# Down products of a routed expert layer with w2 held in TensorE and the activations streamed, results turned by VectorE and put back into rows through DRAM

## Chip, cores and metric

One NeuronCore of a Trainium2 chip runs the whole program. The metric is device microseconds (us) from start to end of one execution; lower is better. An execution's own time is a little longer than the span that the profile covers, which goes from the first to the last instruction of the program.

## What is computed

A recurrence per head gives rows `x` (3072 tokens of 384 numbers), and an expert layer with one expert per token follows. Only the second part is touched:

```python
logits = x @ w_gate + modality_bias[modality_id]
e_idx = argmax(logits, axis=1)
...
for e in range(8):
    mask = e_idx == e
    h = maximum(x[mask] @ w1[e], 0)               # 384 -> 1024
    out[mask] = gate_w[mask, None] * (h @ w2[e])  # 1024 -> 384
```

With the inputs used, 2663 tokens go to one expert, 409 to another, and none to the other six.

## The kernel before, in words

Until about 122 us the recurrence runs in 24 steps. Its rows are scattered by expert to a DRAM buffer `xs` (GpSimd, L635), and a table in SBUF (`table`, L512) says for each block of rows which expert it has, where it starts, and whether its expert differs from that of the block before (`tab[:, 2]`). The expert layer then runs over `seq` (L892): blocks 0 to 4 of 512 rows, block 5 of 416 rows (the narrow block, `BQ`), and half a block (`HO`, 128 rows). With these inputs blocks 0 to 4 and the half block have the large expert, and block 5 the small one.

Each block has an up stage (`blk_up`, L699) and a down stage (`blk_down`, L720), both in eight steps f of 128 hidden columns. Each fp32 product is made of three fp32r products: a rounded part and a rest of either operand (`wh`, `wl` of the weights; `xh`, `xo` and `hh`, `hl` of the activations). The **up** stage holds a 128x128 piece of w1 in TensorE and streams the block's 512 (or 416) columns: 9 matmuls a step. Its result goes to one of three PSUM banks in turn (`UPB`, L697), so step f reuses the bank of step f-3. ScalarE makes `hh` from it (L714) and VectorE `hl` (L716). The **down** stage holds 128 columns of `hh` or `hl` in TensorE and streams 384 columns of w2: 3 matmuls for each of 4 groups of 128 rows, 12 a step, into the banks pY, pX, pK and pU. The narrow block has three such groups and 32 rows left, for which two matmuls with 64 and 32 held columns do (L732, L733); `blk_sum` adds their two halves. Right after the down stage `blk_out` (L743) scales each group on ScalarE straight from PSUM into `ot` (L756), and GpSimd scatters `ot` to the rows of the output (L747).

The schedule is written by hand: every engine runs its instructions in the order in which the program issues them. What stands around the blocks:

- `w_split` (L223): ScalarE rounds two steps' worth of the next block's weights into `wh` (L225), then VectorE (w1) or GpSimd (w2; VectorE in block 0 and the last) makes `wl` (L226). For w1 it stands behind steps f = 1, 3, 5, 7 of the up stage, in block 1 behind f = 0, 2, 4, 6 of its down stage; for w2 behind f = 1, 3, 5, 7 of the down stage.
- `blk_raw` (L644): SyncE (SP) loads the weights of a block ahead into `raw[0]` (w1) and `raw[1]` (w2), each in two halves, if the expert differs; if not, the load is issued with a false condition. For k = 0 SP first reads two values of `tab` (L646, L647). Block 3's `raw[0]` is issued after the down stage of block 1 (L964); those of later blocks stand ahead of a down stage (L942).
- `rows_load` (L652): SP loads a block's rows into `xl` with four DMAs of 192 KB in pieces of 384 bytes. `blk_t` (L671), issued at f = 0 of the block before's down stage, turns them with three VectorE transposes (L666) and makes `xh` and `xo`.
- `guard` (L400): eight checks of the decay inputs on ScalarE, two passes each (L403, L404), spread over blocks 2 to 5 by a step count `s` (`tend`, L882).

Of the kernel before, what the change touches and what calls it, by code (L numbers as in the profile page):

```python
# [9 lines left out]
F32 = mybir.dt.float32  # L10
# [24 lines left out]
NA = 2  # L35
NB = 4
NQ = NA + NB
NBX = 8
NH = 1
NHX = E * (JT - 1)  # L40
# [18 lines left out]
def kernel(ctx: ExitStack, tc: tile.TileContext, rkw, vt, wf, cst, mid, wg, bias, w1, w2, out):  # L59
# [3 lines left out]
    dp = ctx.enter_context(tc.tile_pool(name="dp", bufs=1, space=bass.MemoryType.DRAM))  # L63
    ps = ctx.enter_context(tc.tile_pool(name="ps", bufs=1, space=bass.MemoryType.PSUM))
    xs = dp.tile([XROWS, XW], F32, name="xs")


    cp.tile([P, 32], F32, name="pad0")
# [443 lines left out]
    def table(ph):  # L512
# [12 lines left out]
        def rows(o, nb, cu, f, base, unit=BT):  # L525

            sh = [P, nb, E]
            bc = lambda v: v[:, None, :].to_broadcast(sh)
            ib = ibk[:, 0:nb]
            at = C_EQ if ph == 0 else 0  # L530
            cm, c2 = rcol(at, nb, E), rcol(at + nb * E, nb, E)
            ct = C_TAB if ph == 0 else 2 * nb * E
            te, tr = rcol(ct, nb), rcol(ct + nb, nb)
            t2 = wt((ph, o), "t2", [P, NHX], 1)[:, 0:nb]
            tt(out=cm, in0=bc(cu[:, 1:E + 1]), in1=ib[:, :, None].to_broadcast(sh), op=ALU.is_le)
            vec.tensor_reduce(out=te, in_=cm, axis=AX.X, op=ALU.add)
            if f is not None:
                tt(out=c2, in0=cm, in1=bc(f), op=ALU.mult)
                vec.tensor_reduce(out=tr, in_=c2, axis=AX.X, op=ALU.add)
                tt(out=t2 if base is None else tr, in0=ib, in1=tr, op=ALU.subtract)  # L540
            if base is not None:
                t = rcol(ct + 2 * nb, nb)
                ts(out=t, in0=te, scalar1=-float(E), scalar2=None, op0=ALU.add)
                tt(out=cm, in0=bc(i8), in1=t[:, :, None].to_broadcast(sh), op=ALU.is_equal)
                tt(out=c2, in0=cm, in1=bc(base), op=ALU.mult)
                vec.tensor_reduce(out=t2, in_=c2, axis=AX.X, op=ALU.add)
                if f is not None:
                    tt(out=t2, in0=tr, in1=t2, op=ALU.add)
            yield

            vec.scalar_tensor_tensor(out=tr, in0=te, scalar=float(RS // unit), in1=t2, op0=ALU.mult, op1=ALU.add)
            ts(out=tab[:, 1, o:o + nb], in0=tr, scalar1=float(unit), scalar2=float(DUMMY), op0=ALU.mult, op1=ALU.min)
            es = tabe[:, o:o + nb]
            ts(out=es, in0=te, scalar1=float(E - 1), scalar2=None, op0=ALU.min)
            ts(out=tab[:, 0, o:o + nb], in0=te, scalar1=float(E - 1), scalar2=None, op0=ALU.min)
            prev = e0f if o == 1 else tabe[:, o - 1:o] if o == NA else tabe[:, NQ - 1:NQ]
            for c0, c1, pv in ((0, 1, prev), (1, nb, es[:, 0:nb - 1]))[0:nb]:
                vec.scalar_tensor_tensor(out=tab[:, 2, o + c0:o + c1], in0=te[:, c0:c1], scalar=float(E - 1), in1=pv,
                                         op0=ALU.min, op1=ALU.not_equal)
            yield  # L560

        n, g, f, cu = (rcol(C_VEC + k * E, E + k // 3) for k in range(4))
# [135 lines left out]

    def blk_up(q, f):  # L699
        xh, xo = (t[:, :, 0:width(q)] for t in X["x", q][0:2])  # L700
        pp = pt(f"u{q}_{f}", UPB[(q * FC + f) % 3] if isinstance(q, int) and q else f"pS{f % 2}", (P, BT))[:, 0:width(q)]
        n = 0
        for c in range(KC):
            for wsrc, xsrc in ((wh, xh), (wh, xo), (wl, xh)):
                nc.tensor.matmul(out=pp, lhsT=wsrc[0][:, f, c * P:(c + 1) * P], rhs=xsrc[:, c], start=(n == 0), stop=(n == 3 * KC - 1))  # L705
                n += 1
        w = width(q)
        h2 = bp["h"].tile([P, 2 * BT], F32R, tag="h2", name=f"h{q}_{f}", bufs=FC)
        hh, hl = h2[:, 0:w], h2[:, BT:BT + w]
        cuts = ((0, w, BT),)  # L710
        if w % P:
            wf = w - w % P
            cuts = ((wf, w, w), (0, wf, BT))
        nc.scalar.activation(out=hh, in_=pp, func=AF.Relu)  # L714
        for c0, c1, o in cuts:
            nc.vector.scalar_tensor_tensor(out=h2[:, o:o + c1 - c0], in0=pp[:, c0:c1], scalar=0.0, in1=hh[:, c0:c1].bitcast(F32), op0=ALU.max, op1=ALU.subtract)  # L716
        X["h", q, f] = (hh, hl)
        X["hx", q, f] = h2

    def blk_down(q, f):  # L720
        if f == 0:
            X["y", q] = [pt(f"d{q}_{j}", ("pY", "pX" if isinstance(q, int) else "pT", "pK", "pU")[j], (P, DM)) for j in range(JT)]
        hh, hl = X["h", q, f]
        w, last = width(q), f == FC - 1
        for j in range(w // P):
            for n, (hsrc, wsrc) in enumerate(((hh, wh), (hh, wl), (hl, wh))):
                nc.tensor.matmul(out=X["y", q][j], lhsT=hsrc[:, j * P:(j + 1) * P], rhs=wsrc[1][:, f],  # L727
                                 start=(f == 0 and n == 0), stop=(last and n == 2))
        n = w % P
        if n:  # L730
            h2, c0, y = X["hx", q, f], w - n, X["y", q][JT - 1]
            nc.tensor.matmul(out=y[0:2 * n], lhsT=h2[:, c0:c0 + 2 * n], rhs=wh[1][:, f], start=(f == 0), stop=last, skip_group_check=True)  # L732
            nc.tensor.matmul(out=y[0:n], lhsT=h2[:, c0:c0 + n], rhs=wl[1][:, f], start=False, stop=last, skip_group_check=True)  # L733

    def blk_sum(q):
        n = width(q) % P
        y = X["y", q][JT - 1]
        t = bp["p"].tile([P, DM], F32, tag="t", name=f"t{q}", bufs=1)[0:n]
        nc.scalar.copy(out=t, in_=y[n:2 * n])
        nc.vector.tensor_tensor(out=t, in0=y[0:n], in1=t, op=ALU.add)  # L740
        X["y", q][JT - 1] = t

    def blk_out(q, js=range(JT), own=None, late=None):  # L743
        xg = X["xg", q]

        def write(j, n, ot):
            ins = nc.gpsimd.indirect_dma_start(  # L747
                out=out[:, :], out_offset=bass.IndirectOffsetOnAxis(ap=xg[0:n, j, 1:2].bitcast(I32), axis=0),
                in_=ot[0:n], in_offset=None, bounds_check=NT - 1, oob_is_err=False)
            if isinstance(q, int):  # L750
                rows_apart("out", ins)

        for j in js:
            ot = own or bp["p"].tile([P, DM], F32, tag="ot", name=f"ot{q}_{j}", bufs=4)
            n = min(P, width(q) - j * P)
            nc.scalar.activation(out=ot[0:n], in_=X["y", q][j][0:n], func=AF.Copy, scale=xg[0:n, j, 0:1])  # L756
            if late is None:
                write(j, n, ot)
            else:
                late.append(lambda a=(j, n, ot): write(*a))  # L760
# [128 lines left out]
            next(X["f"], None)  # L889

    late = []
    seq = [*range(NQ), *range(HO, HO + NH)]  # L892
    for n, q in enumerate(seq):
        nxt, nxt2 = (seq[n + d] if n + d < len(seq) else None for d in (1, 2))
        if q >= HO:
            for k in range(2):
                half_up(q, k)
                if n == NQ and k == 0:
                    blk_out(NQ - 1, (JT - 1,))
            if nxt is not None:  # L900
                half_t(nxt)
            half_down(q)
# [5 lines left out]
        if q > 1:  # L908
            load(nxt)
        for f in range(FC):  # L910
            s = 2 * FC * q + f
            blk_up(q, f)
            if s == 2:
                logits(NU - 1)
# [9 lines left out]
                hook_b(1)  # L924
            if q == 1 or s == FC - 1:
                drain(1, lambda h: nc.gpsimd.tensor_copy(out=pj, in_=h), X["h", q, f][0])
            if q == 1 and f > 3:
                if f > 4:
                    nc.gpsimd.tensor_copy(out=pj, in_=X["h", q, f][0][0:1, 0:1].bitcast(F32))
# [12 lines left out]
        if q >= NA and nxt2 is not None:  # L942
            blk_raw(nxt2, 0)
        for f in range(FC):
            s = 2 * FC * q + FC + f
            blk_down(q, f)
            if f == 0:
                (blk_t if nxt < HO else half_t)(nxt)
            if q == 1 and f % 2 == 0:
                w_split(0, f // 2)  # L950
            if f % 2:
                w_split(1, f // 2, eng=nc.vector if q in (0, NQ - 1) else None)
            if q == 2 and f in (3, 5):
                next(tab1)
            if q == 0:
# [5 lines left out]
                if f == 1:  # L961
                    pad_rows()
            tend(s)
        if q == 1:  # L964
            blk_raw(nxt2, 0)
        if q >= 1 and nxt2 is not None:
            blk_raw(nxt2, 1)
        blk_out(q, range(width(q) // P), late=late if q == 0 else None)
        if q == NQ - 1:
            blk_sum(q)  # L970


    def more_blocks():
# [27 lines left out]
    def any_decay():  # L1001
# [42 lines left out]
        with tc.tile_pool(name="gmoe", bufs=1) as gp:  # L1044
# [16 lines left out]
            with tc.For_i(0, E, 1) as e:  # L1061
# [3 lines left out]
                with tc.For_i(0, NU, 1) as n:  # L1065
# [25 lines left out]
                        nc.scalar.activation(out=hT[:, f], in_=ph[:, 0:P], func=AF.Relu)  # L1091
                    for f in range(FC):
                        nc.tensor.matmul(out=py[:, 0:DM], lhsT=hT[:, f], rhs=raw[1][:, f], start=(f == 0), stop=(f == FC - 1))
                    nc.scalar.activation(out=ot, in_=py[:, 0:DM], func=AF.Copy, scale=sm[:, 3:4])
                    nc.gpsimd.indirect_dma_start(out=out[:, :], out_offset=bass.IndirectOffsetOnAxis(ap=ixi, axis=0),
                                                 in_=ot, in_offset=None, bounds_check=NT - 1, oob_is_err=False)

# [10 lines left out]
def _layout(inp):  # L1108
# [14 lines left out]
    for hh in range(2):  # L1123
# [19 lines left out]
        "wg": np.ascontiguousarray(wg),  # L1143
        "bias": np.ascontiguousarray(inp["moe_modality_bias"]),
        "w1": np.ascontiguousarray(np.asarray(inp["moe_w1"]).reshape(E, P, KC, FC, P).transpose(0, 1, 3, 2, 4)).reshape(E, P, FC * DM),
        "w2": np.ascontiguousarray(np.asarray(inp["moe_w2"]).reshape(E, FC, P, DM).transpose(0, 2, 1, 3)).reshape(E, P, FC * DM),
    }


# [11 lines left out]
```

## Time and profile before

| | |
|---|---|
| median of 3 runs | 337.2 us (337.2 to 337.48) |
| the profiled execution's own time | 337.43 us |
| span that its profile covers | 335.7 us |
| mean granted TensorE clock | 0.995 of full speed |
| busy: PE / PEld / DVE / ACT / POOL | 322.5 / 293.2 / 213.7 / 204.1 / 196.2 us |
| DMA | 58.66 MB, mean 175 GB/s |

PE is TensorE, PEld its loading of held operands, DVE VectorE, ACT ScalarE, POOL GpSimd, SP SyncE. Matmuls are pipelined: the duration of one (384 columns: about 0.33 us) is longer than the distance between the starts of two, so a stage's cost is read from its length.

### The profile page before, as it was taken

Reading aid. Unit: us, or ns where it says so; the run is one execution under the profiler, and the core shown is the slowest. Engines: PE = TensorE matmul, PEld = TensorE weight load, DVE = VectorE, ACT = ScalarE, POOL = GpSimd, SP = SyncE. Lnnn points to the kernel's source line nnn. Section 1 sums busy time; section 2 is a strip of 40 time slices with the busy share of each in tenths; the row PEclk is TensorE's granted clock in tenths of the full one; section 3 lists DMA queues with packets and bytes.
Section 4 is the critical chain, followed back from the end, with each engine's and each line's share of the span. In section 5 each row is a group of like instructions: output and inputs, shape, how many; then the busy total and the mean of one; then the engine's idle time right before and its main releaser. Section 6 shows DMA issues by size and latency. Waiting matters only on the chain. (4 is left out here: it accounts for less than half of the span.)

```text
span 335.7 us, 10127 instructions
## 1 busy us (share of the span) xinstructions
PE 322.5 (96%) x3942; PEld 293.2 (87%) x3943; DVE 213.7 (64%) x376; ACT 204.1 (61%) x467; POOL 196.2 (58%) x226
## 2 busy tenths in 40 slices
PE   7899999998999999999999999999999999999992
PEld 3688999988899897899889988997899889999992
DVE  6999999999999665795334965924550564054230
ACT  3897799787588775642422866737755855732150
POOL 7998889889999884676460880255034604440041
PEclk9999999999999999999999999999999999999998
DMA  7997898977898512426354046017444853360020
GB/s 270 407 353 242 283 287 275 305 240 225 291 324 237 176 54 96 94 110 228 124 162 158 1 128 204 8 65 201 152 166 164 230 215 97 95 211 5 0 78 27
DMA packets 35586, 58.66 MB, mean 175 GB/s; under 512 B 17297, under 2 KB 22089, under 8 KB 35528
## 3 DMA queue, kind: packets, MB, share of 16 engines
q1 hardware_dynamic: 32424, 48.45, 46.0%
q0 software_dynamic: 3104, 9.47, 7.5%
q8 instruction: 33, 0.54, 0.7%
q14 instruction: 25, 0.20, 0.2%
HBM read 57.86 MB, written 12.67 MB: 210 GB/s over the span
## 5 line engine op out<-in xcount | busy, mean ns | idle before, releaser
L226 POOL TENSOR_TENSOR wl<-raw,wh 128x768 fp32r<-128x768 f32 x20 | 39.0, 1954 | 74.4 <-ACT wh L225 74.3
L225 ACT CAST wh<-raw 128x768 fp32r<-128x768 f32 x48 | 39.4, 832 | 39.5 <-PE pU_d L727 16.9
L716 DVE SCALAR_TENSOR_TENSOR h<-pS_u,h 128x512 fp32r<-128x512 f32 (+2 forms) x39 | 23.1, 608 | 39.7 <-ACT h L714 29.0
L747 POOL DMA_INDIRECT out<-ot,xg x24 | 24.7, 1030 | 30.7 <-ACT ot L756 25.2
L705 PE MATMUL pS_u<-xh,wh 128*128 128x512 f32 (+1 forms) x102 | 39.8, 390 | 0.7 <-issue 0.5
L226 DVE TENSOR_TENSOR wl<-raw,wh 128x768 fp32r<-128x768 f32 x28 | 31.0, 1113 | 14.7 <-ACT wh L225 14.4
L705 PE MATMUL pS_u<-xo,wh 128*128 128x512 f32 (+1 forms) x102 | 39.2, 384 | 0.0
L705 PE MATMUL pS_u<-xh,wl 128*128 128x512 f32 (+1 forms) x102 | 39.2, 384 | 0.0
L714 ACT ACTIVATE h<-pS_u 128x512 fp32r<-128x512 f32 (+1 forms) x34 | 19.7, 586 | 27.6 <-PE pS_u L705 23.9
L727 PE MATMUL pX_d<-wh,h 128*128 128x384 f32 x96 | 32.3, 337 | 0.0
L727 PE MATMUL pY_d<-wh,h 128*128 128x384 f32 x96 | 32.2, 335 | 0.0
L727 PE MATMUL pK_d<-wh,h 128*128 128x384 f32 x96 | 32.1, 334 | 0.0
L635 POOL DMA_INDIRECT xs<-xp,posT x24 | 26.2, 1090 | 9.4 <-issue 7.1
L243 POOL TENSOR_TENSOR K<-in,B 128x512 f32<-128x512 f32 x24 | 28.4, 1185 | 4.2 <-PE pK L318 2.3
L304 POOL TENSOR_TENSOR G<-in 128x512 f32<-128x512 f32 x24 | 30.6, 1275 | 0.0
L293 DVE TENSOR_TENSOR_SCAN B<-in,pX_d 128x516 f32<-128x516 f32 x24 | 29.3, 1220 | 1.8 <-DMA in<-rkw 1.8
L296 DVE TENSOR_TENSOR_SCAN E<-in,pX_d 128x516 f32<-128x516 f32 x24 | 29.5, 1229 | 0.8
L727 PE MATMUL pU_d<-wh,h 128*128 128x384 f32 x80 | 26.7, 334 | 0.0
L383 PE MATMUL pY<-v,A 128*64 128x48 f32 x368 | 25.2, 222 | 0.0
L716 DVE SCALAR_TENSOR_TENSOR h<-pT_u,h 128x512 fp32r<-128x512 f32 (+2 forms) x17 | 9.6, 577 | 24.3 <-ACT h L714 24.2
L345 DVE TENSOR_TENSOR A<-pS,m 128x768 f32<-128x768 f32 x24 | 22.7, 948 | 2.4 <-PE pS L343 2.2
L383 PEld LDWEIGHTS pY<-v,A 128*64 128x64 f32 x368 | 23.7, 138 | 0.0
(239 smaller groups left out, 860.6 us busy)
## 6 DMA issues: line engine op xcount, KB each, us to landing
raw<-w SPq DMA_DIRECT2D x24, 768.0 KB
in<-rkw SPq DMA_DIRECT2D x23, 512.0 KB
v<-vt SPq DMA_DIRECT2D x24, 288.0 KB
in<-rkw SPq DMA_DIRECT2D x23, 258.5 KB
wg<-wf SPq DMA_DIRECT2D x8, 576.0 KB
xl<-xs SPq DMA_DIRECT2D x20, 192.0 KB
raw<-w SPq DMA_DIRECT2D x16, 192.0 KB
xs<-zt SPq DMA_DIRECT2D x12, 193.0 KB
```

The lines of the kernel that those rows point to most:

```text
L225: nc.scalar.copy(out=wh[k][:, sl], in_=raw[k][:, sl])
L226: (eng or (nc.vector, nc.gpsimd)[k]).tensor_tensor(out=wl[k][:, sl], in0=raw[k][:, sl], in1=wh[k][:, sl].bitcast(F32), op=ALU.subtract)
L243: nc.gpsimd.tensor_tensor(out=wt(a, "K", [P, 4, P]), in0=quarters(k), in1=quarters(T["B", a][:, 1:517])[:, :, 1:129], op=ALU.mult)
L293: nc.vector.tensor_tensor_scan(out=Bt[:, 516:0:-1], data0=w[:, 516:0:-1], data1=d1[:, 516:0:-1], initial=0.0, op0=ALU.mult, op1=ALU.max)
L296: nc.vector.tensor_tensor_scan(out=Et, data0=w[:, 0:516], data1=d1[:, 1:2].to_broadcast([P, 516]), initial=1.0, op0=ALU.mult, op1=ALU.max)
L304: nc.gpsimd.tensor_tensor(out=wt(a, "G", [P, 512]), in0=r, in1=k, op=ALU.mult)
L383: nc.tensor.matmul(out=yh[64:P, g, sw, hh], lhsT=A[:, hh, g, 1 + sw], rhs=vs[:, g, hh] if sw else v[:, h * D:(h + 1) * D], start=new and n ...
L635: rows_apart("xs", nc.gpsimd.indirect_dma_start(out=xs[:, :], out_offset=bass.IndirectOffsetOnAxis(ap=posT[:, n:n + 1], axis=0), in_=T["xp ...
L705: nc.tensor.matmul(out=pp, lhsT=wsrc[0][:, f, c * P:(c + 1) * P], rhs=xsrc[:, c], start=(n == 0), stop=(n == 3 * KC - 1))
L716: nc.vector.scalar_tensor_tensor(out=h2[:, o:o + c1 - c0], in0=pp[:, c0:c1], scalar=0.0, in1=hh[:, c0:c1].bitcast(F32), op0=ALU.max, op1=A ...
L727: nc.tensor.matmul(out=X["y", q][j], lhsT=hsrc[:, j * P:(j + 1) * P], rhs=wsrc[1][:, f], start=(f == 0 and n == 0), stop=(last and n == 2))
L747: ins = nc.gpsimd.indirect_dma_start(out=out[:, :], out_offset=bass.IndirectOffsetOnAxis(ap=xg[0:n, j, 1:2].bitcast(I32), axis=0), in_=ot[ ...
```

## The change

The blocks run in the order 0, 1, 2, 3, 5, 4, half. In all but block 4 (`TURNED`) the down stage holds 128x128 pieces of w2 and streams the block's columns of `hh` and `hl`: 9 matmuls a step of 512 columns (416 in the narrow block), into three banks. The result has the 384 columns of w2 on partitions, so `blk_turn` turns it in 32x32 blocks on VectorE (three transposes from PSUM) and SP writes it with four DMAs, in pieces of 384 bytes, to a DRAM buffer `yd`; `blk_back` loads it as rows into `yr`. Both stand right behind the down stage, ahead of the `blk_raw` of L964. `blk_out` of a turned block moves to f = 4 of the next block's up stage and reads `yr`. The columns of w2 are reordered on the host to suit; block 4 and the half block undo that in the output access of `blk_out`. The narrow block's `hl` is made by one VectorE instruction in place of two, `blk_sum` goes, and the flags of expert changes follow the new order.

```diff
+ORDER = (*range(NQ - 2), NQ - 1, NQ - 2)
+TURNED = ORDER[:-1]
...
+    yd = {q: dp.tile([BT, DM], F32, name=f"yd{q}") for q in TURNED}
...
     def blk_down(q, f):
...
+        if turned:
+            for c in range(KC):
+                for n, (wsrc, hsrc) in enumerate(((wh, hh), (wl, hh), (wh, hl))):
+                    nc.tensor.matmul(out=X["y", q][c][:, 0:width(q)], lhsT=wsrc[1][:, f, c * P:(c + 1) * P], rhs=hsrc,
+                                     start=(first and n == 0), stop=(last and n == 2))
+            return
+        for j in range(JT):
             for n, (hsrc, wsrc) in enumerate(((hh, wh), (hh, wl), (hl, wh))):
                 nc.tensor.matmul(out=X["y", q][j], lhsT=hsrc[:, j * P:(j + 1) * P], rhs=wsrc[1][:, f],
...
+    def blk_turn(q):
+        nb = width(q) // 32
+        yt = bp["m"].tile([P, NXB, KC, 32], F32, tag="xt", name=f"yt{q}", bufs=1)
+        for c in range(KC):
+            nc.vector.transpose(out=yt[:, 0:nb, c], in_=X["y", q][c][:, 0:width(q)].rearrange("p (b t) -> p b t", t=32))
+        for i in range(4):
+            nc.sync.dma_start(out=yd[q][0:width(q), XC * i:XC * i + XC].rearrange("(b t) c -> t b c", t=32),
+                              in_=yt[32 * i:32 * i + 32, 0:nb].rearrange("p b m r -> p b (m r)"))
+
+    def blk_back(q):
+        w = width(q)
+        j, n = divmod(w, P)
+        yr = bp["p"].tile([P, JT, DM], F32, tag="yr", name=f"yr{q}", bufs=1)
+        nc.sync.dma_start(out=yr[:, 0:j], in_=yd[q][0:j * P].rearrange("(j p) c -> p j c", p=P))
         if n:
...
+            nc.sync.dma_start(out=yr[0:n, j], in_=yd[q][j * P:w])
+        X["y", q] = [yr[:, j] for j in range(JT)]
...
-    seq = [*range(NQ), *range(HO, HO + NH)]
+    seq = [*ORDER, *range(HO, HO + NH)]
...
+            if n and f == 4:
+                blk_out(seq[n - 1], range(-(-width(seq[n - 1]) // P)), late=late if n == 1 else None)
...
             tend(s)
+        if q in TURNED:
+            blk_turn(q)
+            blk_back(q)
         if q == 1:
             blk_raw(nxt2, 0)
         if q >= 1 and nxt2 is not None:
             blk_raw(nxt2, 1)
-        blk_out(q, range(width(q) // P), late=late if q == 0 else None)
-        if q == NQ - 1:
-            blk_sum(q)
+        if q not in TURNED:
+            blk_out(q, range(JT - 1))
...
-        "w2": np.ascontiguousarray(np.asarray(inp["moe_w2"]).reshape(E, FC, P, DM).transpose(0, 2, 1, 3)).reshape(E, P, FC * DM),
+        "w2": np.ascontiguousarray(np.asarray(inp["moe_w2"]).reshape(E, FC, P, 4, KC, 32).transpose(0, 2, 1, 4, 3, 5)).reshape(E, P, FC * DM),
```

## Rows read from the trace of the kernel before

**Rows 1.** The page: span and TensorE's busy time.

```profile
span 335.7 us, 10127 instructions
...
PE 322.5 (96%) x3942; PEld 293.2 (87%) x3943; DVE 213.7 (64%) x376; ACT 204.1 (61%) x467; POOL 196.2 (58%) x226
```

**Rows 2.** TensorE by stage: start:end, length, busy (count), clock, DMA share, GB/s.

```profile
174.28:190.94 16.66, 16.66 (x97) 1.00 0.38 114
190.94:207.31 16.37, 16.37 (x74) 1.00 0.58 169
...
223.97:241.17 17.20, 16.66 (x73) 1.00 0.58 172
...
290.87:304.55 13.68, 13.68 (x75) 1.00 0.41 130
304.55:320.00 15.45, 15.45 (x90) 1.00 0.01 2
```

**Rows 3.** Groups of instructions: busy us, mean ns of one, idle before.

```profile
L705 PE MATMUL pS_u<-xh,wl 128*128 128x512 f32 x87 | 33.9, 390 | 0.0
...
L727 PE MATMUL pY_d<-wl,h 128*128 128x384 f32 x48 | 16.1, 335 | 0.0
```

**Rows 4.** Timeline of ScalarE at the start of block 3 (start, length).

```profile
224.96 1.25 ACT L403 ACTIVATE jk<-wg,glo 128x1152 bf16<-128x1152 f32 x1
...
227.60 0.56 ACT L756 ACTIVATE ot<-pY_d,xg 128x384 f32<-128x384 f32 x1
...
229.45 1.09 ACT L714 ACTIVATE h<-pS_u 128x512 fp32r<-128x512 f32 x2
```

**Rows 5.** Timeline of TensorE in the same place.

```profile
229.91 0.39 PE L705 MATMUL pT_u<-xh,wl 128*128 128x512 f32 x1
230.84 0.50 PE L705 MATMUL pS_u<-xh,wh 128*128 128x512 f32 x1 [0.54 <-issue]
```

**Rows 6.** Timeline of VectorE, end of block 1 and start of block 2.

```profile
180.82 1.64 DVE L666 STREAM_TRANSPOSE xt<-xl 128x512 f32<-128x512 f32 x2 [4.94 <-DMA xl<-xs]
...
188.74 5.12 DVE L226 TENSOR_TENSOR wl<-raw,wh 128x768 fp32r<-128x768 f32 x2
194.44 0.69 DVE L716 SCALAR_TENSOR_TENSOR h<-pS_u,h 128x512 fp32r<-128x512 f32 x1 [0.59 <-ACT h L714]
...
196.68 0.96 DVE L226 TENSOR_TENSOR wl<-raw,wh 128x768 fp32r<-128x768 f32 x1
```

**Rows 7.** Timeline of ScalarE in the up stage of block 2.

```profile
195.82 0.83 ACT L225 CAST wh<-raw 128x768 fp32r<-128x768 f32 x1
197.37 0.60 ACT L714 ACTIVATE h<-pS_u 128x512 fp32r<-128x512 f32 x1 [0.72 <-PE pS_u L705]
```

**Rows 8.** Timeline of SP: block 2's rows, then block 3's weights.

```profile
172.64 2.10 SPq L661 DMA_DIRECT2D xl<-xs  x4
...
188.84 6.82 SPq L220 DMA_DIRECT2D raw<-w  x4
```

**Rows 9.** Timeline of ScalarE in the up stage of block 0.

```profile
128.38 0.84 ACT L225 CAST wh<-raw 128x768 fp32r<-128x768 f32 x1 [0.48 <-DMA raw<-w]
```

**Rows 10.** Timeline of SP in the same place.

```profile
128.28 0.62 SPq L220 DMA_DIRECT2D raw<-w  x2
129.02 0.40 SPq L865 DMA_DIRECT2D xs<-zt  x1
133.52 1.97 SPq L661 DMA_DIRECT2D xl<-xs  x4
```

**Rows 11.** SP's waits from 126 to 140 us: total, times, longest.

```profile
SPq L661 <- DMA xs<-zt: 3.3, 1, 3.3
```

**Rows 12.** DMA traffic from 133 to 141 us in 40 slices of 0.2 us.

```profile
GB/s 0 0 0 0 0 0 0 23 84 94 205 317 300 279 317 250 192 163 146 192 238 271 267 226 170 99 74 42 6 0 0 0 0 0 0 0 0 0 0 0
```

**Rows 13.** SP's reads of the table (L646): min/median/max ns, first and last start.

```profile
L646 SPq TENSOR_LOAD <-tab x6: 267/275/534, 126.7 to 267.5; - x6
```

**Rows 14.** Groups of instructions on VectorE and ScalarE.

```profile
L666 DVE STREAM_TRANSPOSE xt<-xl 128x512 f32<-128x512 f32 x12 | 9.9, 852 | 4.9 <-DMA xl<-xs 4.9
...
L756 ACT ACTIVATE ot<-pK_d,xg 128x384 f32<-128x384 f32 x6 | 3.5, 580 | 0.0
```

**Rows 15.** Timeline of ScalarE behind the last full stage.

```profile
322.35 0.47 ACT L739 COPY t<-pU_d 32x384 f32<-32x384 f32 x1
322.92 0.60 ACT L782 ACTIVATE h<-pS_u 128x512 fp32r<-128x512 f32 x1
```

More of the change, by code (lines that the diff above doesn't have):

```diff
@@ L555, in rows @@
             ts(out=tab[:, 0, o:o + nb], in0=te, scalar1=float(E - 1), scalar2=None, op0=ALU.min)
[L556 to L559, printed above, removed]
+            if o == NA:
+                first = ((slice(0, 1), tabe[:, o - 1:o]), (slice(1, 4, 2), es[:, 0:2]), (slice(2, 3), es[:, 3:4]))
+            else:
+                first = ((slice(0, 1), e0f if o == 1 else tabe[:, ORDER[-1]:ORDER[-1] + 1]),)
+            to = tab[:, 2, o:o + nb]
+            for at, pv in first:
+                vec.scalar_tensor_tensor(out=to[:, at], in0=te[:, at], scalar=float(E - 1), in1=pv, op0=ALU.min, op1=ALU.not_equal)
             yield
@@ L700, in blk_up @@
         xh, xo = (t[:, :, 0:width(q)] for t in X["x", q][0:2])
-        pp = pt(f"u{q}_{f}", UPB[(q * FC + f) % 3] if isinstance(q, int) and q else f"pS{f % 2}", (P, BT))[:, 0:width(q)]
+        pp = pt(f"u{q}_{f}", UPB[(ORDER.index(q) * FC + f) % 3] if isinstance(q, int) and q else f"pS{f % 2}", (P, BT))[:, 0:width(q)]
         n = 0
@@ L709, in blk_up @@
         hh, hl = h2[:, 0:w], h2[:, BT:BT + w]
[L710 to L713, printed above, removed]
         nc.scalar.activation(out=hh, in_=pp, func=AF.Relu)
-        for c0, c1, o in cuts:
-            nc.vector.scalar_tensor_tensor(out=h2[:, o:o + c1 - c0], in0=pp[:, c0:c1], scalar=0.0, in1=hh[:, c0:c1].bitcast(F32), op0=ALU.max, op1=ALU.subtract)
+        nc.vector.scalar_tensor_tensor(out=hl, in0=pp, scalar=0.0, in1=hh.bitcast(F32), op0=ALU.max, op1=ALU.subtract)
@@ L717, in blk_up @@
         X["h", q, f] = (hh, hl)
-        X["hx", q, f] = h2
     def blk_down(q, f):
+        turned = q in TURNED
         if f == 0:
-            X["y", q] = [pt(f"d{q}_{j}", ("pY", "pX" if isinstance(q, int) else "pT", "pK", "pU")[j], (P, DM)) for j in range(JT)]
+            X["y", q] = [pt(f"d{q}_{j}", ("pY", "pX" if isinstance(q, int) else "pT", "pK", "pU")[j], (P, BT if turned else DM))
+                         for j in range(KC if turned else JT)]
         hh, hl = X["h", q, f]
-        w, last = width(q), f == FC - 1
@@ L725, in blk_down @@
-        for j in range(w // P):
+        first, last = f == 0, f == FC - 1
+        if turned:
[5 more added lines that the diff above has]
+        for j in range(JT):
             for n, (hsrc, wsrc) in enumerate(((hh, wh), (hh, wl), (hl, wh))):
@@ L727, in blk_down @@
                 nc.tensor.matmul(out=X["y", q][j], lhsT=hsrc[:, j * P:(j + 1) * P], rhs=wsrc[1][:, f],
-                                 start=(f == 0 and n == 0), stop=(last and n == 2))
-        n = w % P
-        if n:
-            h2, c0, y = X["hx", q, f], w - n, X["y", q][JT - 1]
-            nc.tensor.matmul(out=y[0:2 * n], lhsT=h2[:, c0:c0 + 2 * n], rhs=wh[1][:, f], start=(f == 0), stop=last, skip_group_check=True)
-            nc.tensor.matmul(out=y[0:n], lhsT=h2[:, c0:c0 + n], rhs=wl[1][:, f], start=False, stop=last, skip_group_check=True)
@@ L735, in blk_sum @@
[L735 to L741, printed above, removed]
+                                 start=(first and n == 0), stop=(last and n == 2))
+    def blk_turn(q):
[6 more added lines that the diff above has]
+                              in_=yt[32 * i:32 * i + 32, 0:nb].rearrange("p b m r -> p b (m r)"))
@@ L755, in blk_out @@
             n = min(P, width(q) - j * P)
-            nc.scalar.activation(out=ot[0:n], in_=X["y", q][j][0:n], func=AF.Copy, scale=xg[0:n, j, 0:1])
+            y, o = X["y", q][j][0:n], ot[0:n]
+            if q not in TURNED:
+                y, o = y.rearrange("p (m a r) -> p m a r", m=KC, r=32), o.rearrange("p (a m r) -> p m a r", m=KC, r=32)
+            nc.scalar.activation(out=o, in_=y, func=AF.Copy, scale=xg[0:n, j, 0:1])
             if late is None:
@@ L898 @@
                 if n == NQ and k == 0:
-                    blk_out(NQ - 1, (JT - 1,))
+                    blk_out(ORDER[-1], (JT - 1,))
             if nxt is not None:
@@ L910 @@
         for f in range(FC):
-            s = 2 * FC * q + f
+            s = 2 * FC * n + f
             blk_up(q, f)
@@ L944 @@
         for f in range(FC):
-            s = 2 * FC * q + FC + f
+            s = 2 * FC * n + FC + f
             blk_down(q, f)
@@ L951 @@
             if f % 2:
-                w_split(1, f // 2, eng=nc.vector if q in (0, NQ - 1) else None)
+                w_split(1, f // 2, eng=nc.vector if n in (0, NQ - 1) else None)
             if q == 2 and f in (3, 5):
@@ L967 @@
             blk_raw(nxt2, 1)
-        blk_out(q, range(width(q) // P), late=late if q == 0 else None)
-        if q == NQ - 1:
-            blk_sum(q)
+        if q not in TURNED:
+            blk_out(q, range(JT - 1))
     def more_blocks():
@@ L1093, in any_decay @@
                         nc.tensor.matmul(out=py[:, 0:DM], lhsT=hT[:, f], rhs=raw[1][:, f], start=(f == 0), stop=(f == FC - 1))
-                    nc.scalar.activation(out=ot, in_=py[:, 0:DM], func=AF.Copy, scale=sm[:, 3:4])
+                    nc.scalar.activation(out=ot.rearrange("p (a m r) -> p m a r", m=KC, r=32),
+                                         in_=py[:, 0:DM].rearrange("p (m a r) -> p m a r", m=KC, r=32), func=AF.Copy, scale=sm[:, 3:4])
                     nc.gpsimd.indirect_dma_start(out=out[:, :], out_offset=bass.IndirectOffsetOnAxis(ap=ixi, axis=0),
```

## The prediction

> **What bounds it now.** The page first: TensorE is busy for 322.5 of 335.7 us [rows 1]. That alone says little, since a matmul of 384 columns is booked with 335 ns and one of 512 with 390 ns [rows 3], and they overlap. So I cut the expert layer into stages at the first matmul of each and read their lengths [rows 2]. A full block's down stage has 96 matmuls in 16.66 us, one per 0.1735 us; its up stage has 72 in 16.37 us, one per 0.2274 us, or 2.046 us a step f. The clock stands at 1.00 in all of them. Up and down stages follow each other without a gap up to 320 us, so there the program is as long as TensorE's instructions plus its stalls. One stage has a stall: block 3's up stage takes 17.20 us, and TensorE starts step 3 at 230.84 where 230.1 would follow on [rows 2, 5].
>
> **The gain on TensorE.** Turned, a full block's down stage is 72 matmuls of 512 columns, the form of the up stage: 16.37 in place of 16.66 us, 0.29 less. Columns times matmuls are the same (36,864); what goes is the fixed part of 24 matmuls. Four blocks: 1.16 us. The narrow block's 88 matmuls in 15.45 us become 72 of 416 columns, and its up stage, which has just these, took 13.68 [rows 2]: 1.77 less. Sum 2.93 us.
> The Trainium skill (TensorE: Matmul & The Clock Gate, section Back-to-back issue gap) gives N/2.4 + 2.5 ns for the isolated gap. By it the two sums would be about 0.3 and 1.6 us, some 1.9 in all; the rows show some 14 ns beside the columns, so the rows' 2.93 stands.
>
> **The stall in block 3 goes.** Behind block 2's down stage ScalarE does a guard pair (224.96 to 227.60), four scalings (227.60 to 229.45), and only then the first two `hh` [rows 4]. Step 3 wants the PSUM bank of step 0 and is late. With `blk_out` moved to f = 4, the first `hh` can start at 227.6, 1.85 us sooner, and `hl` of 0.69 us ends before 230.1. Gain: 17.20 − 16.37 = 0.83 us.
>
> **The new wait, behind block 1.** Program order on SP becomes: four writes to `yd`, the load back from it, the table reads, then block 3's `raw[0]`. SP waits for the writes to land ahead of the load, as it did for another write of its own queue [rows 11]. Block 3 has the expert of block 2, so that load moves nothing; yet ScalarE's rounding of w1 waits for it. Block 0 shows this: the load issued with a false condition at 128.28 let the cast go at 128.38, after 0.48 us of waiting [rows 9, 10]. In block 2's up stage the cast (195.82) stands behind step 1 and ahead of `hh` of step 2 (197.37) [rows 7]; before, SP had issued the first half at 188.84 [rows 8], so nothing waited. Now, in times of the trace of before:
> - VectorE ends its w1 splits at 188.74 + 5.12 = 193.86 [rows 6]; they are late because block 2's rows landed only at 180.82. The three transposes queue behind them. From PSUM there is no row. Nearest are two of SBUF in 1.64 us, 852 ns each [rows 6, 14]: 2.45 for three. Below, 1.9, by the 0.69 of an instruction that reads PSUM; above, 2.6. I take 2.45: 196.3.
> - The writes: four DMAs of 192 KB in 384-byte pieces. No row shows such a write. Below: 772 KB written by one DMA, issued at 129.02 and landed by 133.52, 4.5 us [rows 10]. Nearest in form: four loads of the same pieces, issued from 133.52, whose data runs from 134.4 to 138.6 [rows 10, 12], 5.1 us, and with half a microsecond to land 5.6. Above: the same loads under other traffic, 172.64 to 180.82, 8.2 us [rows 6, 8]. I take 5.6, the same pieces on quiet engines, plus 0.1 to wake SP: 202.0.
> - One issue to load back, 0.4 [rows 10]; the table reads up to the weight load, 1.6 (126.7 to 128.28) [rows 10, 13]; 0.1 to release ScalarE: the cast starts at 204.1.
> - Behind it the cast 0.83, the rest on VectorE 0.96, `hl` of step 2 0.69 [rows 6, 7]: 206.6. Three banks rotate, so step 5 waits for this; undisturbed it starts at 190.94 + 5 × 2.046 = 201.17. Stall 5.4 us. `hh` of steps 2 and 3, VectorE's second split and later guards queue behind the same cast, but steps 3 and 4 use banks that are free.
> - VectorE's backlog hangs on the scatters of block 1's up stage, which move forward by one block's gain; the end of block 1's down stage moves by two. So 0.3 more: **5.7 us**. With all lower ends 4.1, with all upper ends 8.5.
> The Trainium skill (DMA: Bandwidth & Descriptors, section Anatomy of one DMA) puts a DMA at 2 us plus bytes at 436 GB/s. By it, with issues 0.55 us apart, the writes would land 4.1 us after the first issue and the total be near 337.9. The quiet loads, longer in the rows, decide.
>
> **What else it adds.** In the narrow block's up stage steps are 13.68/8 = 1.71 us, and a guard pair of 2.64 [rows 4] stands behind step 1. Step 1's end 3.4, `hh` 0.75 later, cast 0.75, pair 2.64, `hh` and `hl` of step 2 about 1.2: 8.8 against the 8.55 at which step 5 wants the bank. An estimate: 0.3 us.
> At nothing I cost: the transposes behind blocks 0, 2, 3 and 5 (VectorE has 6.1 us, three steps, before a bank is missed; 2.45 fit; behind block 1 the first `hl` ends at 197.0, and step 3 starts at 197.08); the scalings at f = 4 (four of 0.58 [rows 14], 1.9 us overlapped; the `hh` behind them is first read a stage later, so they may even wait some 10 us for `yr`; beyond that, one for one); the loads of `raw[1]` and `xl`, about 8 us later on SP but needed a stage of 13.7 us or more later (their cover gone, ScalarE would wait within the down stage, where TensorE has all its `hh`); the other expert's weights a block sooner (the same number of loads); one VectorE instruction more in the table. In the tail `blk_sum`'s ScalarE copy of 0.47 goes ahead of an `hh` [rows 15], but TensorE goes on without a gap there.
> **Sum:** −2.93 − 0.83 + 5.7 + 0.3 = +2.2 us. The profiled execution, 337.43, would become 339.7; it stands 0.23 above the median of 337.2, which becomes **339.4**.
>
> **Rivals.**
> *No new wait* (0.18). The cast is released in time: SP does not hold the false load behind the round trip. It decides at a cast start of 201.17 − 2.48 = 198.7. Then 337.2 − 3.46 = 333.7, faster. For it: the load moves no data. Against: rows 9 show such a load gating the cast, and no row of a write allows the round trip in 2.4 us.
> *A shorter wait* (0.14). VectorE's last two splits took 5.12 us where one can take 0.96 [rows 6]. Were block 2's rows to land sooner, the transposes would start up to 3.2 us earlier: stall 2.5, 336.2; half way it is 337.8. For it: the output writes of block 0, which run beside that load, move later. Against: the load itself waits for the scatters.
> *Slow small writes* (0.08). The pieces are written as a read and a write of their surroundings, and the data takes twice its 4.2 us [rows 12]: 343.6. Beside it, the Trainium skill (DMA: Bandwidth & Descriptors, section Specifications) says that below 512 bytes the engines do read-modify-write; no row here shows it.
> *The form is dearer than in the up stage*: w2's pieces might not follow each other at 0.2274 us. Nothing in the rows parts the two, so I give it no chance of its own.
>
> **Numbers.** The forecast has 0.60, with 337.8 to 342.2 as its own range. A measurement of this kernel can tell about 0.2% (0.7 us) from no change. Faster: the first rival and half of the second, 0.25. Same: the other half and the forecast's short end, 0.09. Slower: the rest and the third, 0.66. The range takes in the first rival and leaves out the third: 333.5 to 342.0.
>
> **What would show it.** Down stages of 16.4 us (full) and 13.7 (narrow). Block 2's up stage near 22 us, with one gap at step 5, ScalarE's cast there idle until SP's weight load, and SP's wait for `yd`; block 3's up stage at 16.4. Wrong, if that cast starts at its step; if the gap is elsewhere (the scalings at f = 4 holding TensorE would show the `yr` load landing late); or if down stages still take 16.7.

## The result and the profile after

The changed kernel takes 341.28 us (median of 6 runs, 339.88 to 343.05) against 337.2 (336.84 to 337.49): a ratio of 1.0113, 95% interval 1.0077 to 1.0148. It is slower, as forecast, and by 4.1 us where 2.2 were forecast. Its profiled execution took 339.88 us, 2.45 more than that of before.

The page of the changed kernel, span, busy time and granted clock by 40 slices of the span, beside [rows 1]:

```profile
span 338.0 us, 9945 instructions
...
PE 321.2 (95%) x3830; PEld 280.5 (83%) x3831; DVE 221.6 (66%) x382; ACT 203.8 (60%) x466; POOL 195.6 (58%) x226
...
PEclk9999999999999999999999997999999999999999
```

Fewer matmuls, a longer span. TensorE by stage (start:end, length, busy, clock, DMA share, GB/s; beside [rows 2]): block 1 down, block 2 up, block 2 down, block 3 up, narrow up, narrow down.

```profile
175.23:191.55 16.32, 16.32 (x74) 1.00 0.49 134
191.55:213.96 22.41, 18.22 (x74) 0.92 0.60 159
213.96:230.28 16.32, 16.32 (x73) 1.00 0.52 181
230.28:246.60 16.32, 16.32 (x73) 1.00 0.79 231
...
262.92:276.62 13.70, 13.70 (x73) 1.00 0.73 231
276.62:290.18 13.56, 13.56 (x73) 1.00 0.55 160
```

Turned down stages are now about as long as up stages of the same block (16.32 and 13.56 us, where 16.66 and 15.45 stood), block 3's up stage has lost its stall, and all of that is outweighed by one stage: block 2's up stage has grown from 16.37 to 22.41 us, and its clock stands at 0.92. TensorE's timeline shows where (start, length):

```profile
201.52 0.39 PE L711 MATMUL pT_u<-xh,wl 128*128 128x512 f32 x1
206.10 0.50 PE L711 MATMUL pS_u<-xh,wh 128*128 128x512 f32 x1 [4.19 <-DVE h L717]
...
207.04 0.63 PE L711 MATMUL pS_u<-xh,wh 128*128 128x512 f32 x1
207.46 0.63 PE L711 MATMUL pS_u<-xo,wh 128*128 128x512 f32 x1
```

Step 5 starts 4.58 us behind the last matmul of step 4. Less one distance of 0.23 that is 4.35 us of idle time, released by VectorE's `hl` of step 2. From about 206.7 on the matmuls follow each other at 0.42 us in place of 0.23: TensorE is at the lower of its two levels, 1.2 GHz. The stage's 6.09 us beyond 16.32 are 4.35 of waiting and 1.74 of half clock.

Three timelines and a list of waits tell what `hl` of step 2 waited for. SP, beside [rows 8, 10]:

```profile
196.29 2.35 SPq L744 DMA_DIRECT2D yd<-yt  x4
201.49 0.38 SPq L751 DMA_DIRECT2D yr<-yd  x1
203.47 1.57 SPq L223 DMA_DIRECT2D raw<-w  x4
```

VectorE, beside [rows 6]:

```profile
191.85 2.59 DVE L229 TENSOR_TENSOR wl<-raw,wh 128x768 fp32r<-128x768 f32 x1
194.37 0.70 DVE L742 STREAM_TRANSPOSE yt<-pY_d 128x512 f32<-128x512 f32 x1
...
196.19 0.65 DVE L717 SCALAR_TENSOR_TENSOR h<-pS_u,h 128x512 fp32r<-128x512 f32 x1
196.79 0.69 DVE L717 SCALAR_TENSOR_TENSOR h<-pT_u,h 128x512 fp32r<-128x512 f32 x1
204.48 0.96 DVE L229 TENSOR_TENSOR wl<-raw,wh 128x768 fp32r<-128x768 f32 x1 [7.00 <-ACT wh L228]
```

ScalarE's longest wait in the same stretch (total, times, longest), beside [rows 9]:

```profile
ACT wh L228 <- DMA raw<-w: 6.9, 1, 6.9
```

and the cast that waited, beside [rows 7]:

```profile
203.62 0.83 ACT L228 CAST wh<-raw 128x768 fp32r<-128x768 f32 x1 [6.86 <-DMA raw<-w]
204.36 1.08 ACT L716 ACTIVATE h<-pS_u 128x512 fp32r<-128x512 f32 x2
```

It is the chain of the forecast. VectorE ends its splits, turns (1.8 us), SP writes and waits (5.2 us from the first issue to the load back), reads the table, issues the load that moves nothing (203.47), and 0.15 us later the cast starts; two `hh` stand in line behind it.

### The profile page after: what moved, and what is told of

Read it like the earlier page. It is cut to its first block, busy times and chain, and to the rows that moved or that the text cites. A ratio compares the mean times of both kernels' runs of the same rounds, so it can differ in the third digit from the quotient of the medians.

```text
span 338.0 us, 9945 instructions
## 1 busy us (share of the span) xinstructions
PE 321.2 (95%) x3830; PEld 280.5 (83%) x3831; DVE 221.6 (66%) x382; ACT 203.8 (60%) x466; POOL 195.6 (58%) x226
## 5 line engine op out<-in xcount | busy, mean ns | idle before, releaser
L760 POOL DMA_INDIRECT out<-ot,xg x24 | 25.9, 1078 | 66.8 <-ACT ot L772 62.3
L717 DVE SCALAR_TENSOR_TENSOR h<-pS_u,h 128x512 fp32r<-128x512 f32 (+1 forms) x34 | 22.7, 673 | 35.0 <-ACT h L716 35.0
L711 PE MATMUL pS_u<-xh,wh 128*128 128x512 f32 (+1 forms) x102 | 40.6, 398 | 4.4 <-DVE h L717 4.4
L641 POOL DMA_INDIRECT xs<-xp,posT x24 | 24.5, 1020 | 11.1 <-issue 8.2
L730 PE MATMUL pY_d<-h,wh 128*128 128x512 f32 (+1 forms) x80 | 30.5, 382 | 0.0
L730 PE MATMUL pX_d<-h,wh 128*128 128x512 f32 (+1 forms) x80 | 30.5, 382 | 0.0
L730 PE MATMUL pK_d<-h,wh 128*128 128x512 f32 (+1 forms) x80 | 30.5, 382 | 0.0
L711 PEld LDWEIGHTS pS_u<-xh,wh 128*128 128x128 f32 x102 | 19.5, 191 | 8.9 <-DVE h L717 5.5
L252 ACT ACTIVATE pU_st<-pU_st,B 128x48 f32<-128x48 f32 x80 | 22.0, 275 | 3.0 <-PE pU_st L358 0.6
```

Source lines behind the costliest of these rows:

```text
L641: rows_apart("xs", nc.gpsimd.indirect_dma_start(out=xs[:, :], out_offset=bass.IndirectOffsetOnAxis(ap=posT[:, n:n + 1], axis=0), in_=T["xp ...
L730: nc.tensor.matmul(out=X["y", q][c][:, 0:width(q)], lhsT=wsrc[1][:, f, c * P:(c + 1) * P], rhs=hsrc, start=(first and n == 0), stop=(last ...
L760: ins = nc.gpsimd.indirect_dma_start(out=out[:, :], out_offset=bass.IndirectOffsetOnAxis(ap=xg[0:n, j, 1:2].bitcast(I32), axis=0), in_=ot[ ...
```

## The experiments

All ratios are to the kernel before, run on the same chip between the variants; there its median was 338.73 us in the first group of four and 338.16 in the second, with most executions within some 4 us of each other. Much of that spread lies in the recurrence: block 0's up stage starts anywhere from 122.5 to 126.3 us in these profiles. So beside each ratio stands the stretch from the first matmul of block 0's up stage to the first of the half block's down stage, which the change is about. It was 202.4 us before and 204.5 in the changed kernel's first profile. The times expected of the first four start from the first measurement's 337.2; put on that scale by their ratios, the four come out at 332.9, 332.7, 334.9 and 335.9 us.

| variant | ratio (95% interval) | that stretch, us | block 2 up, us |
|---|---|---|---|
| weights first | 0.9873 (0.983 to 0.9917) | 198.4 | 16.35 |
| casts late | 0.9867 (0.9788 to 0.9945) | 198.4 | 16.32 |
| narrow block alone | 0.9931 (0.9902 to 0.996) | 200.7 | 16.36 |
| before, scalings late | 0.996 (0.9925 to 0.9994) | 201.6 | 16.36 |
| writes twice | 1.0225 (1.0146 to 1.0305) | 209.2 | 27.11 |
| weights between | 0.994 (0.9906 to 0.9975) | 200.4 | 18.56 |
| changed, again | 1.0068 (1.0028 to 1.0108) | 205.1 | 23.31 |

### Weights first

```diff
+        if q == 1:
+            blk_raw(nxt2, 0)
         if q in TURNED:
             blk_turn(q)
             blk_back(q)
-        if q == 1:
-            blk_raw(nxt2, 0)
```

> One edit to the changed kernel: block 3's w1 load (with its table reads) is issued on SP ahead of block 1's transposes and round trip instead of behind them. Theory (the false load waits on SP for the round trip, ScalarE's cast waits for it, TensorE runs out of PSUM banks and then also loses its clock): block 2's up stage falls from 22.41 us to 16.4, its clock stays at 1.00, and the whole comes to 337.2 - 2.9 - 0.8 = 333.5 us, between 333 and 334.5, with runs as close together as those of the kernel before (0.7 us). Rival A (the transposes ahead of VectorE's first hl, or the scalings at f = 4 waiting for yr, make the gap): they are unchanged here, so the stage stays at 20 us or more and the time at 340 to 342. Rival B (the added DMA traffic slows the program and spreads the runs): time and spread stay as in the changed kernel, 340 to 343.

Measured: 0.9873, 334.3 us in the median. TensorE's block 2 up and down stages, and block 3's up stage:

```profile
193.68:210.03 16.35, 16.35 (x74) 1.00 0.51 125
210.03:226.35 16.32, 16.32 (x74) 1.00 0.81 274
226.35:242.67 16.32, 16.32 (x74) 1.00 0.77 224
```

The gap is gone, with the transposes, the round trip and its traffic all still there, as SP's timeline shows:

```profile
199.00 2.36 SPq L744 DMA_DIRECT2D yd<-yt  x4
204.01 0.38 SPq L751 DMA_DIRECT2D yr<-yd  x1
```

ScalarE's waits in that up stage name the other candidate, the scalings at f = 4:

```profile
ACT ot L772 <- DMA yr<-yd: 2.6, 1, 2.6
```

They do wait 2.6 us for `yr`, and TensorE doesn't notice: rival A falls in both halves. Rival B falls by the time. The spread says nothing either way: these executions lie 3.2 us apart, where 0.7 were expected, but those of the kernel before, run beside them, lay some 4 us apart. Against the kernel before, this version is faster by 1.3%, and its stretch is some 6 us shorter than the changed kernel's: two lines moved turn a loss into a gain.

### Casts late

```diff
-            if q != 1 and f % 2 and nxt < HO:
+            if q not in (1, 2) and f % 2 and nxt < HO:
                 w_split(0, f // 2)
+            if q == 2 and f > 4:
+                w_split(0, f - 5)
+                if f == FC - 1:
+                    w_split(0, 3)
```

> One edit to the changed kernel: in block 2's up stage the four roundings of w1 stand behind steps 5, 6, 7 and 7 instead of 1, 3, 5 and 7. SP's order and its round trip are unchanged. Theory: the wait for the false load is still there but falls on an instruction behind which no bank is due: no gap in block 2's up stage (16.4 us), time 333 to 335. Rival A (transposes or late yr): the stage stays at 20 us or more. Rival C (SP's wait delays something else as well, rows or w2 for the next block): the stage is whole, but a gap appears in block 2's down stage or at the start of block 3, and the time stays above 336.

Measured: 0.9867, 332.5 us in the median of four executions (332.3, 332.4, 332.7 and 337.3). SP is where it was in the changed kernel:

```profile
195.24 2.35 SPq L744 DMA_DIRECT2D yd<-yt  x4
200.34 0.38 SPq L751 DMA_DIRECT2D yr<-yd  x1
202.31 1.57 SPq L223 DMA_DIRECT2D raw<-w  x4
```

and the stages are whole, 16.32 us in both of block 2 and in block 3's up stage. Block 2's up stage:

```profile
189.86:206.18 16.32, 16.32 (x74) 1.00 0.37 101
```

SP's late arrival at the load costs nothing by itself; it costs because a cast that needs the load stands ahead of `hh` of step 2 on ScalarE. Rival C falls.

### Narrow block alone

```diff
-TURNED = ORDER[:-1]
+TURNED = (NQ - 1,)
...
-            if n and f == 4:
+            if n and f == 4 and seq[n - 1] in TURNED:
...
-            blk_out(q, range(JT - 1))
+            blk_out(q, range(JT - 1 if q == ORDER[-1] else JT), late=late if q == 0 else None)
```

> One part of the change alone: the new order, and only the narrow block turned; blocks 0 to 4 hold activations as before and are scaled right behind their down stage. The host's column order stays. The prediction's terms: the narrow block's down stage 13.6 us in place of 15.45, 1.8 less; full down stages 16.66; block 3's stall of 0.8 stays, since the scalings stand where they stood; no round trip behind block 1, so no gap in block 2. Time 337.2 - 1.8 = 335.4, between 334.8 and 336. Rival (the order itself costs, by the small expert's weights arriving during the guard loads or by the full block's larger tail): 336.5 or more, with a gap in the fourth or fifth up stage or a longer stretch behind the last down stage.

Measured: 0.9931, a gain of 2.3 us with an interval from 1.4 to 3.3; the stretch is shorter by 1.7. Block 3's up stage, then the narrow block's two:

```profile
224.76:241.96 17.20, 16.66 (x74) 1.00 0.69 219
258.62:272.35 13.73, 13.73 (x73) 1.00 0.76 226
272.35:285.91 13.56, 13.56 (x73) 1.00 0.01 2
```

Block 3's up stage stays at 17.20 us, as it should where the scalings stay, and the order itself costs little: of the 1.9 us that the narrow block's down stage gains, 1.7 are left in the stretch. The four full blocks together gain less on TensorE (1.4 us, below) than this one.

### Scalings late in the kernel before

```diff
+            if n and f == 4:
+                blk_out(seq[n - 1], late=late if n == 1 else None)
...
-        blk_out(q, range(width(q) // P), late=late if q == 0 else None)
         if q == NQ - 1:
+            blk_out(q, range(width(q) // P))
             blk_sum(q)
```

> One edit to the kernel before: the scalings of a block (all but the last) move from right behind its down stage to f = 4 of the next block's up stage, still read from PSUM. Theory (block 3's stall comes from a guard pair and four scalings ahead of the first hh): block 3's up stage falls from 17.20 to 16.4 us and the time to 336.4, between 336.0 and 336.8. Rival (the stall is the guard pair's alone): the stage stays near 17.2 and the time at 337.2.

Measured: 0.996 (0.9925 to 0.9994), a gain of 1.4 us whose interval reaches from 0.2 to 2.5; the stretch gives 0.9. Block 3's up stage:

```profile
224.11:240.47 16.36, 16.36 (x74) 1.00 0.59 156
```

The guard pair is still there, so the rival falls. The stall of 0.83 us [rows 2, 5] was the pile of guard pair and scalings [rows 4], and this part of the gain needs nothing else of the change.

### Writes twice

```diff
-        for i in range(4):
+        for i in range(4 if q != 1 else 8):
+            i %= 4
             nc.sync.dma_start(out=yd[q][0:width(q), XC * i:XC * i + XC].rearrange("(b t) c -> t b c", t=32),
```

> The changed kernel with block 1's four writes to its buffer issued a second time behind the first, each waiting for its first to land; nothing else. Theory (idle time in block 2's up stage follows the landing of the writes one for one, and TensorE's clock falls behind it): the load of block 3's w1 is issued 4 us later, the gap at step 5 grows from 4.4 to about 8.4 us, the clock is at half for 3.4 us or more behind it as in the changed kernel, the stage is 26.5 us or more (22.41 there), and the time 4 us above the changed kernel's in this call. Rival (the gap comes from something else than the writes' landing): the stage stays at 22.4 us.

Measured: 1.0225. SP, then TensorE at the gap, then TensorE in the stretch behind it:

```profile
196.16 5.51 SPq L745 DMA_DIRECT2D yd<-yt  x8
204.60 0.38 SPq L752 DMA_DIRECT2D yr<-yd  x1
```

```profile
209.13 0.80 PE L711 MATMUL pS_u<-xh,wh 128*128 128x512 f32 x1 [7.99 <-DVE h L717]
```

```profile
209.13:217.75 8.62, 8.62 (x28) 0.70 0.97 257
```

The load back comes 8.4 us behind the first issue in place of 5.2, 3.2 later; the idle time is 8.15 us in place of 4.35. Behind it the clock averages 0.70. The stage is 27.11 us, and 27.11 − 16.32 − 8.15 = 2.6 us of that is half clock. The gap has grown by 3.8 us, of which 3.2 are the later landing. The rest lies ahead of the writes: VectorE's splits ended 3.7 us behind the stage's start in place of 2.9, so that the cast came at 16.0 us behind it in place of 12.1. The gap follows these two, one for one within 0.2 us. The stretch is some 4 us longer than in the second profile of the changed kernel (205.1), as expected; the whole is 3.0 us longer by the medians and 5.3 by the ratios.

### Weights between

```diff
             blk_turn(q)
-            blk_back(q)
         if q == 1:
             blk_raw(nxt2, 0)
+        if q in TURNED:
+            blk_back(q)
```

> The changed kernel with block 3's w1 load issued between the four writes and the load back: the cast then waits for the transposes and for the issue of the writes, no longer for their landing. Theory: SP reaches the load some 8.7 us behind block 1's down stage (4.7 transposes done, 2.35 four issues, 1.6 table reads), the cast runs at 8.8, and TensorE's gap at step 5 is 1.0 to 1.5 us in place of 4.4. If the clock falls only behind the long gap, it stays at 1.00 here: stage 17.4 to 17.9 us, time 1 to 1.5 us above the kernel with the weights first, 4 to 5 below the changed kernel in this call. If any gap costs the clock as well, the stage is 19 us or more.

Measured: 0.994, 4.3 us below the changed kernel measured beside it. SP, then TensorE at the gap, then the whole stage:

```profile
195.12 2.35 SPq L744 DMA_DIRECT2D yd<-yt  x4
199.88 0.62 SPq L223 DMA_DIRECT2D raw<-w  x2
```

```profile
200.20 0.39 PE L711 MATMUL pT_u<-xh,wl 128*128 128x512 f32 x1
202.51 0.50 PE L711 MATMUL pS_u<-xh,wh 128*128 128x512 f32 x1 [1.93 <-DVE h L717]
```

```profile
190.22:208.78 18.56, 16.63 (x73) 1.00 0.60 136
```

Idle for 2.1 us where 1.0 to 1.5 were expected, and the stage 18.56 us. SP reached the load 2.4 us behind the last issue of the writes, not 1.6. The two reads of the table account for the difference: here they took 0.73 and 0.63 us, where such reads take 0.27 in the median [rows 13] and in the changed kernel, whose reads come after the writes have landed. That the writes in flight slow them is likely, but not shown. So the stretch is 2.0 us longer than with the weights first, where 1 to 1.5 was expected. The clock question is answered for this execution: behind a gap of 2.1 us it stays at 1.00, and the stage loses little more than the wait (2.2 us).

### The changed kernel again

No edit.

> The changed kernel itself beside its variants. Theory: the time beyond the idle 4.4 us is TensorE at half clock behind the gap, and how long that lasts differs between executions; so the executions' times fall with their mean granted clock (0.993 to 0.982 at the first measurement, 339.9 to 343.1 us), and the mean clock is lower than in the variants without the gap (0.995 to 0.999). Rival (the spread is that of the DMA round trip alone, longer or shorter waits at the same clock): times vary while the mean clock stays above 0.992.

Measured: 1.0068. TensorE at the gap and behind it:

```profile
207.21 0.80 PE L711 MATMUL pS_u<-xh,wh 128*128 128x512 f32 x1 [3.96 <-DVE h L717]
```

```profile
207.21:216.19 8.98, 8.98 (x28) 0.68 0.97 266
```

The wait is the first profile's (4.1 us idle), but the clock averages 0.68 over the 9 us behind it: 2 × 0.32 × 8.98 = 5.7 us at half, where the first profile had 3.4. The stage is 23.31 us, of which 2.9 is half clock. So with the same wait the same kernel loses 1.7 or 2.9 us to the clock. The executions' mean clocks run from 0.982 to 0.993; those of the kernel before, measured beside them, from 0.985 to 0.999, 18 of 21 at 0.994 or more. That part of the theory holds. That the time follows the clock holds only roughly (0.993 with 338.0 us, 0.982 with 342.5, but 0.987 and 0.988 with anything from 339.6 to 342.3): the spread of the recurrence is likely to lie on top.

## Why the prediction was right, and where its sizes were off

**The gain on TensorE**, 2.93 us forecast: four full blocks 4 × (16.66 − 16.32) = 1.36 and the narrow one 15.45 − 13.56 = 1.89, so 3.25. Right, and 0.3 too small: the full stages ran 0.05 us shorter than the up stage that the sum took, and the narrow block's 13.68 us were not 72 matmuls alone, as the forecast had it, but held a small one of another tile (`pR_g`) as well. The 16.32 us are 0.2267 a matmul of 512 columns, as the up stage's rows said. The Trainium skill's N/2.4 + 2.5 ns (TensorE: Matmul & The Clock Gate, section Back-to-back issue gap), by which the gain was near 1.9 (0.24 for the four full blocks, which the forecast wrote as 0.3, and 1.64), does not agree.

**The stall in block 3**, 0.83 forecast: gone (17.20 to 16.32 us), and shown alone by moving the scalings within the kernel before (16.36).

**The wait behind block 1**, 5.7 forecast: right in place, cause and step; mis-sized in two ways that pull apart. The idle time was 4.1 to 4.4. From the stage's start the cast began at 12.1 us in place of 13.5: the transposes took 1.8 (lower end 1.9, taken 2.45), the writes 5.2 with the wake-up (taken 5.7), and the 0.3 for the scatters did not come. The reads and issues fitted (2.0 both). What was missing is a term: TensorE's clock behind the idle time, 1.7 us in one profile and 2.9 in the other. With it the wait costs 6.1 to 7.0 us. The Trainium skill's formula beside the sum (DMA: Bandwidth & Descriptors, section Anatomy of one DMA), by which the writes took 4.1 us, was further off than the loads of the trace; it is fitted there to DMAs issued from GpSimd, and these were SP's.

**The narrow block's guard**, 0.3: right in place, half in size. TensorE starts step 5 of that stage late:

```profile
271.13 0.34 PE L711 MATMUL pS_u<-xh,wl 128*128 128x416 f32 x1
271.43 0.46 PE L711 MATMUL pS_u<-xh,wh 128*128 128x416 f32 x1
```

That is 0.30 us where 0.19 is the distance elsewhere, and the next matmul comes 0.29 later. The stage takes 13.70 us against 13.56 in the down stage of the same form, and 13.66 to 13.73 in all seven profiles of the new order. (That the trace of before has 13.68 as well is a coincidence: there the small matmul stands in this stage, and in the new order it stands in block 4's.) **The edits at nothing** cost nothing that shows in the stretch, the scalings' own wait for `yr` included.

**The sum.** The stretch from block 0 to the half block's down stage grew by 2.0 us in the first profile and 2.7 in the second, against 2.2 forecast. The terms as measured in the first, −3.25 − 0.88 + 6.09 + 0.14, make 2.1. That the forecast came so near is in part luck: a wait taken some 1.4 us too long stood in for the half clock that was left out. Outside the stretch, the profiled execution's start of block 0 was 1.3 us late (124.17 against 122.84). The seven profiles with this program up to there start block 0 anywhere from 122.49 to 126.31 us, so the 1.3 are no fixed cost of the change; whether the change shifts that spread is open. The tail, from the half block's first down matmul to the end, was 1.1 us short: 9.4 us against 10.4. It was 9.4 to 10.1 in all seven profiles of the new order, and 10.4 and 10.8 in the two of the old one, so a part of it may well be a gain of the change, which the forecast had at nothing; its cause stays open. The median's 4.1 lies above the profile's 2.45, and the other executions had lower mean clocks (0.982 to 0.988 against 0.993), which fits. Whether clock alone accounts for the rest of it was not settled: the second measurement gave 1.0068, 2.3 us.

**The rivals.** *No new wait* falls by the cast's 6.86 us of waiting; its price was about right, since the two variants that take the wait away gained 4.0 us in the stretch, against the 3.46 forecast. *A shorter wait* falls as far as its reason goes: VectorE ended its splits 2.9 us into the stage, as in the trace of before. *Slow small writes* falls: writes in pieces of 384 bytes landed in 5.2 us, and twice the data time was asked. The Trainium skill (DMA: Bandwidth & Descriptors, section Specifications) has read-modify-write below 512 bytes; here such writes took 5.2 us until they had landed, about as long as loads in the same pieces (5.1 us to the last data [rows 10, 12]), so no cost of it shows. *The form is dearer* falls too: 0.2267 us a matmul in the turned down stages, as in the up stages.

## What to carry to other kernels

A transfer issued with a false condition moved no data here, and yet whoever needed it waited until the issuing engine got to it. So a round trip through DRAM put ahead of it delays everything behind it on that queue. Put waits that end late behind everything that the issuing engine could send out at once, and place a cast that depends on such a transfer behind the last instruction that frees an accumulator bank. When pricing a stall of a busy TensorE, add the time at half clock that may follow it; and a change that mixes gains and a wait is best tried with the wait taken out by reordering, before it is judged.

## What the runs showed of the hardware

TensorE's clock fell at the long gaps and not at the short one. Behind 2.1 us of idle time it stayed at 1.00; behind 4.1 and 4.4 us it stood at half for 5.7 and 3.4 us (0.68 over 8.98 us, and 0.78 over the 7.86 us from the gap's end to the stage's); behind 8.2 us it averaged 0.70 over 8.62. Each of these is one execution, and the time at half did not follow the gap's length: in the first profile, of 4.4 us, matmuls came at full speed for some 0.6 us behind the gap before the clock fell; behind the gaps of 4.1 and 8.2 us it was at half from the first one on. In each case TensorE had run without a pause for over 50 us before. At half clock a matmul of 512 columns came every 0.42 us. So the price of the stall was not proportional to it: 2.2 us for an idle 2.1, 6.1 to 7.0 for 4.1 to 4.4, and 10.8 for 8.2. The Trainium skill (TensorE: Matmul & The Clock Gate, section HAM oscillation — how this bites in real kernels) says that waits in mid-kernel can take the clock down, so that the work behind them starts slow; the traces with the three long gaps agree (0.68 to 0.78 behind them).

VectorE's transposes from PSUM were cheaper than those from SBUF in the trace of before: 0.67 to 0.72 us a 128x512 tile against 0.85 [rows 14]. The two also differ in the order of their input, so which of these does it is open.
